# A first stage reordered: half loads, one bank per set, and folds moved between two engines

## The chip, the cores and the metric

The kernel runs on one core of a Trainium2 chip. The metric is the device time of one execution in microseconds (us); lower is better. A core has five engines that work through queues of their own and wait for each other by semaphores: TensorE (PE in the profile, with its weight loads as PEld), VectorE (DVE), ScalarE (ACT), GpSimd (POOL) and SyncE (SP, which here only issues DMAs). ACT and POOL issue some DMAs too. A time "at 14.00" is counted from the start of the profiled span.

## The reference

The kernel computes a Fourier mixing layer and then a gated feed-forward layer. The input `x` is 8 batches of 3008 rows of 256 numbers, in float32:

```python
X = np.fft.fft(x, axis=1)            # over 3008 rows
X = np.fft.fft(X, axis=2)            # over 256 columns
x2 = X.real.reshape(24064, 256)
g = x2 @ w_gate                      # 256 -> 1536
out = (g / (1 + exp(-g)) * (x2 @ w_val)) @ w_out   # 1536 -> 256
```

## The kernel before, in words

The real part of the two transforms is a sum of products of cosines and sines. The cosine and sine over the 256 columns are multiplied into the gate and value weights (`Wp` and `Wq`, and `Wm`, a signed copy of `Wq`), so that the transform over rows is all that is left for the data. A row k and its mirror M-k share their products: `P` (even part) and `Q` (odd part) are computed once, and the two rows come out as `P·Wp + Q·Wq` and `P·Wp + Q·Wm`.

The transform over rows is made small by folding. The 3008 rows are split into four residues ("sets", a = 0 to 3); in each, rising rows are added to falling rows (the mirror), then the columns are folded on themselves into even and odd halves (`EOA`, `EOb`, index `eo`). What is left is multiplied on PE with a table of sines and cosines `Tab`, made on the chip from iotas. A batch has a large part A (128 rows per set) and a rest C (60 rows per set, two sets stacked on one tile).

The kernel has two stages.

*The first stage* (code up to `tmp_ctx.close()`, some 20 us) is written out by hand, engine by engine, in program order. It loads batch 0, builds the tables, folds, transforms, and multiplies the first 512 columns of the gate and value weights. Its steps, by the lines that the profile names:

- `x` loads: the four rising sets in one DMA of 1024 KB (L261), four falling sets of 256 KB each, issued in turn by ACT and SP (`fall_a`, L264), the rising rest (`rises_c`, L267, 512 KB), four falling pieces of the rest (`fall_c`, L270), and row 0 through POOL's queue (L404).
- warm-up: 48 matmuls of a zero tile (L306).
- tables: iotas on POOL (L282 to L288), `turns` on POOL (L364), `angles` and `magnitude` on DVE (L368, L372), sines and cosines on ACT (L375, L378), sign copies on ACT (`opposite`, L384; `weigh_ce`, L387). `putA` and `putC` are permutation matrices: an iota and a comparison (L286 and L355 for A, L301 and L406 for C).
- `place` (L438): a float32 matmul with `putA` or `putC` brings the rising rows of one set into the order of the falling ones, in PSUM.
- folds: DVE adds the falling rows to it. `cross` does it for sets 0 and 1 (L447), and `cross_halves` and `half_fold` for sets 2 and 3 and the rest C (L451, L452, L460), `ends` for the one column left over (L455). POOL folds the columns of sets 0 and 1 in `fold_d` (L497), the odd sums for sets 2 and 3 as well, and adds the odd sums up (L570). ACT casts the even ones to bfloat16 (L500).
- transform: `half_folded` (L488) and `folded_c` (L493) on PE into four accumulators `acc[eo][q]`; `row0` (L628) adds the row 0 terms (`heads`, L464 and L465 on POOL) to the two odd accumulators. ACT copies `acc[eo][0]` to SBUF (`even_copy`, L517), and DVE adds and subtracts it from `acc[eo][1]` to give `P` and `Q` (`first_puts`, L646).
- weights: POOL issues the DMAs, which cast to bfloat16 (`load_w`, L394): chunk 0 of gate and value (`W0`), then chunks 1 and 2 into the space of `XA`. PE multiplies chunk 0 with the cosine and sine tables (`first_w`, L505); ACT and DVE copy the result out (L508). The order is gate first, then value.
- `turn_signs` (L345 to L347) and `row_signs` (L357, L358) make small sign columns.

PSUM has eight banks. In the first stage they are taken from the three pools that the second stage uses (`psG` 3, `psV` 3, `psO` 2).

*The second stage* goes over tiles of 512 columns of `P`, `Q` and 12 blocks of the hidden size each. Its order is made before the program runs by a planner: every operation has an engine, a duration, a due time (`SHIFT` and `BIAS` tables) and dependencies, and the planner writes each engine's queue from these. It starts from fixed assumptions on when the first stage's results are there, and knows nothing of the first stage's code. For the first tiles, a block is: PE multiplies `P·Wp` and `Q·Wq` into a gate and a value bank (L1015), ACT applies the gate function (L1050), DVE multiplies (`hp`, L1053); then PE adds `Q·Wm` terms to the same banks for the mirrored rows, and ACT and DVE do the same again (L1071, L1074). Among them stand the products of weight chunks 1 and 2 (L1501, copied out at L1504, L1507, L1510), and POOL makes `Wm` (L512, L1516). The output product is at L1279.

Of the kernel before, what the change touches and what calls it, by code (L numbers as in the profile page):

```python
# [12 lines left out]
F32 = mybir.dt.float32  # L13
I32 = mybir.dt.int32
BF16 = mybir.dt.bfloat16
AF = mybir.ActivationFunctionType
Alu = mybir.AluOpType

@with_exitstack
def kernel(  # L20
# [8 lines left out]
    nc = tc.nc  # L29
    B, M, D = x.shape  # L30
    Dff = moe_w_gate.shape[1]
    P = 128
# [46 lines left out]
    psG = Slots("psG", 3, space=bass.MemoryType.PSUM)  # L79
    psV = Slots("psV", 3, space=bass.MemoryType.PSUM)  # L80
    psO = Slots("psO", 2, space=bass.MemoryType.PSUM)
# [6 lines left out]
    Tab = const.tile([P, 2, 2, 2, NTAB], BF16, name="Tab")  # L88
    halfpi = const.tile([P, 1], F32, name="halfpi")
# [31 lines left out]

    def up_block(b, j, n):
        return rows_at(b, 2 * j - 1, [[2 * D, n], [R * D, 4], [1, 2 * D]])

    def rows_at(b, row, ap):
        return bass.AP(tensor=x.tensor, offset=(b * M + row) * D, ap=ap)
# [118 lines left out]
    Ec0 = tp.tile([P, 2, 2, 1], F32, name="Ec0")  # L245
# [27 lines left out]
    fall_a(3, nc.scalar)  # L273
    fall_a(2, q)
    fall_a(1, nc.scalar)
    fall_a(0, q)
    rises_c(q)
# [8 lines left out]
    nc.gpsimd.iota(putA, pattern=[[-LA, NA], [1, LA]], base=JA - 1, **iota)  # L286
# [6 lines left out]
    for a in range(2):  # L293
        fall_c(1, a, q)
        fall_c(0, a, q)
# [7 lines left out]
    for i in range(4):  # L303
        ps = psO.tile([P, T], F32, name="o")
        for j in range(12):
            nc.tensor.matmul(ps[:, 0:P], sel, sel, start=True, stop=True)  # L306
# [7 lines left out]
    mm_ = col("mm", 4)  # L314
# [28 lines left out]
    def turn_signs():  # L343
        n_ = col("n_", 4, I32)
        vts(n_, mm_, scalar1=0.5, scalar2=0.25, op0=Alu.mult, op1=Alu.add)  # L345
        vts(n_, n_, scalar1=1, scalar2=None, op0=Alu.bitwise_and)
        vts(turn_sign, n_, scalar1=-2.0, scalar2=1.0, op0=Alu.mult, op1=Alu.add)  # L347
# [7 lines left out]
    vts(putA, putA, scalar1=pcol, scalar2=None, op0=Alu.is_equal)  # L355
# [6 lines left out]
    def turns(t1, kf, ch):  # L362
        for i in range(2):
            pts(t1[:, i, :], kf, scalar1=mM[:, 2 * ch + i:2 * ch + i + 1], scalar2=1.0, op0=Alu.mult, op1=Alu.mult)  # L364
# [21 lines left out]
    def weigh_ce():  # L386
        nc.scalar.activation(Tab[:, 1, 1, :, 0:NCE], Tab[:, 1, 1, :, 0:NCE], AF.Copy, scale=wC)  # L387

    def load_w(c, only):
        for i, src in ((0, moe_w_gate), (1, moe_w_val)):  # L390
            if i not in only:
                continue
            w_ = src.rearrange("(no p) f -> p no f", p=P)[:, :, c * T:(c + 1) * T]
            nc.gpsimd.dma_start(out=Wraw[i][:, :, (c - 1) * T:c * T] if c else W0[i], in_=w_)  # L394
# [11 lines left out]
    pts(putC, putC, scalar1=pcol, scalar2=1.0, op0=Alu.is_equal, op1=Alu.mult)  # L406
    nc.gpsimd.memset(sel[0:1, :], 1.0)
# [22 lines left out]
    weigh_ce()  # L430
    opposite(0)

    def place(X, put, n, pools):
        pss = []
        for a in range(n):
            pool, nm = pools[a % len(pools)]
            ps = pool.tile([P, 2, D], F32, name=nm)
            nc.tensor.matmul(ps.rearrange("p q d -> p (q d)"), put, X[:, a].rearrange("p q d -> p (q d)"),  # L438
                             start=True, stop=True)
            pss.append(ps)  # L440
        return pss

    def falling(X, pss, a):
        return (X[:, 7 - a] if len(pss) == 4 else X[:, 2 + a])[:, ::-1]

    def cross(to, X, pss, a):
        vtt(to[:, :, 1:D], pss[a][:, :, 1:D], falling(X, pss, a)[:, :, D - 1:0:-1], op=Alu.add)  # L447

    def cross_halves(to, X, pss, a):
        down = falling(X, pss, a)  # L450
        vtt(to, pss[a][:, :, 1:P + 1], down[:, :, D - 1:P - 1:-1], op=Alu.add)  # L451
        vtt(pss[a][:, :, P:D], pss[a][:, :, P:D], down[:, :, P:0:-1], op=Alu.add)  # L452

    def ends(to, X, pss, a):
        vtt(to, pss[a][:, :, 0:1], falling(X, pss, a)[:, :, 0:1], op=Alu.add)  # L455
# [3 lines left out]
    def half_fold(eo, to, low, pss, a):  # L459
        vtt(to, low[:, :, ::-1], pss[a][:, :, P:D], op=SUMS[eo])  # L460

    def heads(ev, od, CE):

        ptt(CE[:, :, 0, 0, -1:], ev, od, op=Alu.add)  # L464
        ptt(CE[:, :, 0, 1, -1:], ev, od, op=Alu.subtract)  # L465
# [3 lines left out]
    def warm(n):  # L469
        ps = psO.tile([P, T], F32, name="o")  # L470
        for i in range(n):
            nc.tensor.matmul(ps[:, 0:P], sel, sel, start=True, stop=True)

    def start_acc(eo):
        for q, (pool, nm) in enumerate(((psV, "v"), (psG, "g"))):
            acc[eo][q] = pool.tile([P, T], F32, name=nm)
# [7 lines left out]
    def half_folded(eo, a0, first):  # L484
        for q in range(2):
# [9 lines left out]
    def fold_d(eo, a0):  # L495
        F = FA[:, a0:a0 + 2]
        ptt(EOA[eo][a0 // 2], F[:, :, :, P:0:-1], F[:, :, :, P:D], op=SUMS[eo])  # L497

    def half_cast(eo, a0):
        nc.scalar.copy(EOb[:, eo, a0:a0 + 2], EOA[eo][a0 // 2])  # L500
# [18 lines left out]

    psG.at = psV.at = 2  # L520
    psA = place(XA, putA, 4, ((psG, "g"), (psV, "v")))
    warm(8)
    for a in range(2):
        cross(FA[:, a], XA, psA, a)
    for a in range(2):
        ends(Eh[:, a], XA, psA, a)
# [9 lines left out]
    for a in range(2, 4):  # L536
        ends(Eh[:, a], XA, psA, a)
    start_acc(0)
    start_acc(1)
    psC = place(XC0, putC, 2, ((psO, "o"),))  # L540
# [3 lines left out]
    half_cast(0, 2)  # L544
    nc.scalar.activation(Z0.rearrange("p q k d -> p (q k d)"), zero.to_broadcast([P, 6 * P]), AF.Copy)
    opposite(1)
# [19 lines left out]
    fold_d(1, 2)  # L566
    hd = tp.tile([P, 2, 2, 1], F32, name="hd")
    ptt(hd, Eh[:, 0:2], Eh[:, 2:4], op=Alu.add)
    heads(hd[:, 0], hd[:, 1], CEa)
    ptt(EOb[:, 1, 0:2], EOA[1][0], EOA[1][1], op=Alu.add)  # L570
    half_folded(0, 0, True)
    half_folded(0, 2, False)
    cross_halves(FC[:, 0], XC0, psC, 0)
    half_fold(0, EB[:, 0, 0], FC[:, 0], psC, 0)
    folded_c(0, 0)
    copies = [first_w(0, k, 1, p_.tile([P, T], F32, name=n_)) for k, (p_, n_) in enumerate(((psG, "g"), (psV, "v")))]
    cross_halves(FC[:, 1], XC0, psC, 1)
    half_fold(0, EB[:, 0, 1], FC[:, 1], psC, 1)
    folded_c(0, 1)
    od0 = even_copy(0)  # L580
    for a in range(2):
        half_fold(1, EB[:, 1, a], FC[:, a], psC, a)
    for a in range(2):
        ends(Ec0[:, a], XC0, psC, a)
    for a in range(2):
        folded_c(1, a, True)
    half_folded(1, 0, False)
    load_w(1, (1,))
    heads(Ec0[:, 0], Ec0[:, 1], CEc)
    load_w(2, (0, 1))  # L590
    for k in range(2):
        pts(BBc[:, :, 1, k, 0:1], Ec0[:, 1 - k], scalar1=(nsgn, sgn)[k], scalar2=1.0, op0=Alu.mult, op1=Alu.mult)
    nc.gpsimd.iota(kfO, pattern=[[4, GH]], base=1, **iota)
# [70 lines left out]
    tmp_ctx.close()  # L664

# [1099 lines left out]
```

## Time and profile before

| what | value |
|---|---|
| time before, median of 3 runs | 597.46 us (597.39 to 598.78) |
| the profiled execution's own time | 597.77 us |
| its span | 596.0 us |
| PE busy in the span | 590.9 us, 99% |
| DVE, ACT, POOL busy | 568.6, 553.6 and 533.5 us |
| granted PE clock over the span | 1.0 |

The page lists busy times, a chain of waits followed back from the last instruction, and groups of instructions by line. A row of the timeline gives the start, the duration, the engine, the line, what is written from what, the tile's shape, how many instructions are merged, and in brackets the idle time before it with what ended that. Durations of neighbouring instructions of one engine overlap by some 0.08 us on DVE and 0.1 us on ACT, so what an instruction costs its engine is the distance to the next start.

### The profile page before, as it was taken

The page shows a single profiled execution, that of the slowest core. Times are in us where ns is not written, and L with a number is a line of the kernel's source. Part 1 is how long each engine was busy: PE and PEld are TensorE (multiplying, and loading weights), DVE is VectorE, ACT ScalarE, POOL GpSimd, SP SyncE. Part 2 cuts the span into 40 slices and gives each one's busy share as a digit, 9 for nine tenths or more (in the row PEclk, how much of TensorE's full clock was granted, in tenths as well). Part 3 has the DMA queues.
Part 4 walks back from the last instruction along what each step waited for, and adds up shares of the span by engine and source line. Part 5 has one row for each costly group of instructions (what it writes and reads, how often), then busy time and mean ns, then how long its engine had stood idle before and what let it go on. Part 6 is the DMA issues. An engine that isn't in the chain of part 4 may idle for free.

```text
span 596.0 us, 12394 instructions
## 1 busy us (share of the span) xinstructions
PE 590.9 (99%) x4014; PEld 390.6 (66%) x4014; DVE 568.6 (95%) x1062; ACT 553.6 (93%) x1071; POOL 533.5 (90%) x491
## 2 busy tenths in 40 slices
PE   9999999999999999999999999999999999999997
PEld 6456676666666666666666666666666666666686
DVE  9989999999999999999999999999999999999993
ACT  8768989999998899899999999999999999999995
POOL 9979999999999999999899998999889868687782
PEclk9999999999999999999999999999999999999999
DMA  9976772756244255285125122054121103202212
GB/s 251 161 222 229 185 235 71 194 165 222 82 149 126 73 139 137 68 273 159 54 82 168 37 64 63 19 152 143 46 63 37 47 19 88 67 28 63 60 54 81
DMA packets 61070, 68.17 MB, mean 114 GB/s; under 512 B 6744, under 2 KB 48668, under 8 KB 61006
## 3 DMA queue, kind: packets, MB, share of 16 engines
q1 hardware_dynamic: 57422, 64.44, 36.1%
q0 software_dynamic: 3216, 2.36, 2.9%
q8 instruction: 31, 0.51, 0.4%
q10 hardware_dynamic: 368, 0.59, 0.3%
q14 instruction: 33, 0.27, 0.2%
HBM read 40.21 MB, written 35.43 MB: 127 GB/s over the span
## 4 chain that ended last, share of the span: by engine, by line
PE 96%; DVE 0%; ACT 0%; issue 0%
PE o L1279 41%; PE g L1015 27%; PE v L1015 21%; PE g L1453 2%; PE o L1453 2%; PE v L1279 1%; PE o L1501 1%; PE g L622 0%; PE o L622 0%; PE g L1279 0%; PE o L1582 0%; PE g L1650 0%; DVE Wp L508 0%; ACT es L1289 0%; DVE Qt L646 0%
## 5 line engine op out<-in xcount | busy, mean ns | idle before, releaser
L1226 POOL TENSOR_TENSOR hm<-sv 128x1024 bf16<-128x1024 f32 (+2 forms) x137 | 254.7, 1862 | 32.3 <-ACT sv L1202 12.9
L1218 DVE SCALAR_TENSOR_TENSOR sv<-es,v 128x512 f32<-128x512 f32 (+2 forms) x262 | 174.0, 670 | 5.9 <-PE v L1015 4.3
L1279 PE MATMUL o<-Wo,hm 128*128 128x256 bf16 (+1 forms) x1128 | 163.7, 273 | 0.0
L1279 PE MATMUL o<-Wo,hp 128*128 128x256 bf16 (+1 forms) x1104 | 161.1, 272 | 0.0
L1229 DVE TENSOR_TENSOR hp<-sp,v 128x512 bf16<-128x512 f32 (+2 forms) x228 | 151.6, 671 | 1.9 <-PE v L1015 1.1
L1279 PEld LDWEIGHTS <-hm 128*128 128x128 bf16 (+2 forms) x1140 | 111.9, 98 | 58.0 <-issue 0.6
L1279 PEld LDWEIGHTS <-hp 128*128 128x128 bf16 (+2 forms) x1140 | 111.8, 98 | 55.3 <-issue 0.3
L1202 ACT ACTIVATE sv<-g 128x512 f32<-128x512 f32 (+2 forms) x181 | 119.0, 675 | 3.6 <-PE g L1015 3.1
L1127 ACT ACTIVATE sp<-g 128x512 f32<-128x512 f32 (+2 forms) x181 | 112.1, 621 | 5.9 <-PE g L1015 4.0
L1015 PE MATMUL g<-Pt,Wp 128*128 128x512 bf16 (+2 forms) x288 | 107.5, 374 | 0.0
L1015 PE MATMUL v<-Pt,Wp 128*128 128x512 bf16 (+2 forms) x288 | 106.2, 375 | 0.2 <-DVE Wp L508 0.2
L1015 PE MATMUL g<-Qt,Wq 128*128 128x512 bf16 (+2 forms) x288 | 105.4, 375 | 0.1
L1088 ACT ACTIVATE v<-bc,w 128x512 f32<-128x512 bf16 (+2 forms) x139 | 100.3, 726 | 1.9 <-DVE sv L1218 1.0
L1152 DVE SCALAR_TENSOR_TENSOR es<-bc,w,v 128x512 f32<-128x512 bf16 (+2 forms) x135 | 97.9, 732 | 2.1
L1150 ACT ACTIVATE es<-v 128x512 f32<-128x512 f32 (+2 forms) x139 | 86.0, 621 | 3.2 <-PE v L1015 1.6
L1015 PEld LDWEIGHTS <-Wp 128*128 128x128 bf16 x576 | 56.3, 98 | 26.0 <-DVE Wp L508 1.0
L1015 PE MATMUL g<-Qt,Wm 128*128 128x512 bf16 (+2 forms) x195 | 73.1, 376 | 0.0
L1131 DVE SCALAR_TENSOR_TENSOR sg<-bc,w,g 128x512 f32<-128x512 bf16 (+2 forms) x93 | 67.3, 724 | 1.6 <-PE g L1015 1.4
L1235 POOL TENSOR_TENSOR hp<-sp,pp 128x512 bf16<-128x512 f32 (+1 forms) x46 | 57.2, 1245 | 8.0 <-ACT pp L1232 7.8
L1202 ACT ACTIVATE sv<-sg 128x512 f32<-128x512 f32 (+2 forms) x93 | 63.6, 695 | 0.5 <-DVE sg L1195 0.5
L1195 DVE SCALAR_TENSOR_TENSOR sg<-sg,g 128x512 f32<-128x512 f32 (+2 forms) x93 | 61.6, 663 | 0.2
L1015 PEld LDWEIGHTS <-Wq 128*128 128x128 bf16 x437 | 42.7, 98 | 27.5 <-issue 0.4
(218 smaller groups left out, 788.7 us busy)
## 6 DMA issues: line engine op xcount, KB each, us to landing
out_dram<-ev SPq DMA_DIRECT2D x96, 128.0 KB
XA<-in_x_dram SPq DMA_DIRECT2D x30, 256.0 KB
tA<-in_x_dram SPq DMA_DIRECT2D x28, 256.0 KB
XA<-tA SPq DMA_DIRECT2D x14, 512.0 KB
XC<-in_x_dram SPq DMA_DIRECT2D x28, 120.0 KB
tC<-in_x_dram SPq DMA_DIRECT2D x28, 120.0 KB
XC<-tC SPq DMA_DIRECT2D x6, 480.0 KB
bc<-br SPq DMA_DIRECT2D x19, 128.0 KB
```

Source lines behind the costliest of these rows:

```text
L1015: nc.tensor.matmul(ps[:, :n], Wt[:, gv, fs], src[:, :n], start=start, stop=stop, skip_group_check=True)
L1088: nc.scalar.activation(T_[kv][:, :w], bc[t][:, :w], AF.Copy, scale=w0[:, 1, f:f + 1])
L1127: nc.scalar.activation(sp_to()[:, :w], T_[kg][:, :w], AF.Silu)
L1131: nc.vector.scalar_tensor_tensor(T_[keg][:, :w], bc[t][:, :w], w0[:, 0, f:f + 1], T_[kg][:, :w], op0=Alu.mult, op1=Alu.add)
L1150: nc.scalar.activation(T_[kes][:, :w], T_[kv][:, :w], AF.Copy, scale=2.0 if on_pool(u) > 1 else 1.0)
L1152: nc.vector.scalar_tensor_tensor(T_[kes][:, :w], bc[t][:, :w], w0[:, 1, f:f + 1], T_[kv][:, :w], op0=Alu.mult, op1=Alu.add)
L1195: nc.vector.scalar_tensor_tensor(T_[kgm][:, :w], T_[keg][:, :w], 2.0, T_[kg][:, :w], op0=Alu.mult, op1=Alu.subtract)
L1202: nc.scalar.activation(sv()[:, f % 2, w - 1::-1, 1], T_[kgm if by_dve else kg][:, :w], AF.Silu)
L1218: nc.vector.scalar_tensor_tensor(sv()[:, f % 2, w - 1::-1, 0], T_[kes][:, :w], 2.0, T_[kv][:, :w], op0=Alu.mult, op1=Alu.subtract)
L1226: nc.gpsimd.tensor_tensor(hts_(t)[1][:, f - 1:f + 1, :w], sv()[:, :, :w, 1], sv()[:, :, :w, 0], op=Alu.mult)
L1229: nc.vector.tensor_tensor(hts_(t)[0][:, f, :wp], T_[ksp][:, :wp], T_[kv][:, :wp], op=Alu.mult)
L1279: nc.tensor.matmul(st["ps"][:n, j, :], hts[t][minus][:, f, c:c + n], Wo[:, f, :], start=(f == 0), stop=(f == nF - 1))
```

## The change

Everything changed is in the first stage; in the second, each engine's instructions stand in the same order as before, behind a first stage that ends with some small POOL operations moved to its end.

- The rising rows of batch 0 are loaded in two halves of 512 KB (`rises_a`). ACT issues falling sets 3 and 2; SP issues set 1, then the rising rest, then set 0. Row 0 goes through SP's queue between two pieces of the rest, no longer through POOL's.
- The warm-up is 33 matmuls; 5 more stand behind each pair of placements.
- Each set has a PSUM bank of its own: placements of A in banks 4, 5, 0, 1, of C in 6, 7; accumulators in 2, 3 (even) and 6, 7 (odd); the four products of weight chunk 0 in 0, 1, 4, 5. The pools of the second stage are opened behind the first.
- `putA`: its iota goes behind the first `turns` on POOL, and its comparison from DVE to POOL.
- `opposite(0)` stands ahead of `weigh_ce` on ACT, and `opposite(1)` ahead of the clearing of `Z0`.
- `fold_d(0, 0)` stands ahead of the load of the gate weights, chunk 0; the loads of chunks 1 and 2 follow the last `fold_d` without other POOL work between.
- The sum of the odd folds (L570), `hd` and `heads` go from POOL to DVE, behind the folds of C.
- The odd accumulators are finished one after the other, each with its `row0`, and `even_copy(1)` is issued after the first.
- For the value weights, ACT copies `Wp` and DVE `Wq` (before, DVE `Wp` and ACT `Wq`). `first_puts(1)` for tile 0 is issued between the two.
- `turn_signs`, `row_signs`, two small products of `Ec0`, an iota and the setting of `sel` go to the end of the stage.

```diff
-    q.dma_start(out=XA3[:, 0:4, :], in_=up_block(0, 1, P))
+    def rises_a(a):
+        q.dma_start(out=XA3[:, a:a + 2, :], in_=rows_at(0, R * a + 1, [[2 * D, P], [R * D, 2], [1, 2 * D]]))
...
+    rises_a(0)
     nc.scalar.activation(w0[:, 0, 0:1], zero, AF.Silu)
     fall_a(3, nc.scalar)
-    fall_a(2, q)
-    fall_a(1, nc.scalar)
+    rises_a(2)
+    fall_a(2, nc.scalar)
+    fall_a(1, q)
+    rises_c(q)
     fall_a(0, q)
-    rises_c(q)
...
-    nc.gpsimd.iota(putA, pattern=[[-LA, NA], [1, LA]], base=JA - 1, **iota)
...
-    for a in range(2):
-        fall_c(1, a, q)
-        fall_c(0, a, q)
+    fall_c(1, 0, q)
+    q.dma_start(out=XC0[NCR:64 + NCR + 1:64, 2:4, 0], in_=rows_at(0, 0, [[2 * R * D, 2], [R * D, 2], [1, D]]))
+    fall_c(0, 0, q)
+    for hi in (1, 0):
+        fall_c(hi, 1, q)
...
-    vts(putA, putA, scalar1=pcol, scalar2=None, op0=Alu.is_equal)
...
     turns(ti[0], kf, 0)
+    nc.gpsimd.iota(putA, pattern=[[-LA, NA], [1, LA]], base=JA - 1, **iota)
+    pts(putA, putA, scalar1=pcol, scalar2=1.0, op0=Alu.is_equal, op1=Alu.mult)
     turns(ti[1], kf, 1)
     more_iotas()
-    nc.gpsimd.dma_start(out=XC0[NCR:64 + NCR + 1:64, 2:4, 0],
-                        in_=rows_at(0, 0, [[2 * R * D, 2], [R * D, 2], [1, D]]))
     pts(putC, putC, scalar1=pcol, scalar2=1.0, op0=Alu.is_equal, op1=Alu.mult)
-    nc.gpsimd.memset(sel[0:1, :], 1.0)
...
-    weigh_ce()
     opposite(0)
...
-    psA = place(XA, putA, 4, ((psG, "g"), (psV, "v")))
-    warm(8)
+    for a in range(4):
+        place(bA[a], XA, putA, a)
+        if a % 2:
+            warm(5)
...
-    row_signs()
-    load_w(0, (0,))
-    fold_d(0, 0)
-    load_w(0, (1,))
-    fold_d(1, 0)
-    for a in range(2, 4):
-        cross_halves(FA[:, a, :, 1:P + 1], XA, psA, a)
-    for a in range(2, 4):
-        half_fold(0, EOA[0][1][:, a - 2], FA[:, a, :, 1:P + 1], psA, a)
+    fold_d(0, 0)
+    load_w(0, (0,))
+    fold_d(1, 0)
+    load_w(0, (1,))
+    for a in range(2, 4):
+        cross_halves(FA[:, a, :, 1:P + 1], psA[a], XA[:, 7 - a, ::-1])
+        if a == 2:
+            ends_a(0)
+            ends_a(1)
+        half_fold(0, EOA[0][1][:, a - 2], FA[:, a, :, 1:P + 1], psA[a])
...
+    weigh_ce()
     half_cast(0, 0)
...
-    ptt(hd, Eh[:, 0:2], Eh[:, 2:4], op=Alu.add)
+    vtt(EOb[:, 1, 0:2], EOA[1][0], EOA[1][1], op=Alu.add)
+    vtt(hd, Eh[:, 0:2], Eh[:, 2:4], op=Alu.add)
     heads(hd[:, 0], hd[:, 1], CEa)
-    ptt(EOb[:, 1, 0:2], EOA[1][0], EOA[1][1], op=Alu.add)
+    heads(Ec0[:, 0], Ec0[:, 1], CEc)
...
     first_puts(0, od0, (0, 1))
+    for c in copies:
+        c()
     for i in range(2):
+        half_folded(1, 0, False, (i,))
         row0(0, i, acc[1][i])
+        if i == 0:
+            od1 = even_copy(1)
+    copies = [first_w(1, k, 1 - k, one_bank(4 + k)) for k in range(2)]
     copies[0]()
+    first_puts(1, od1, (0,))
     copies[1]()
-    turn_signs()
-    od1 = even_copy(1)
-    copies += [first_w(1, k, k, psO.tile([P, T], F32, name="o")) for k in range(2)]
-    first_puts(1, od1, (0,))
-    for c in copies[2:4]:
-        c()
     first_puts(1, od1, (1,))
     tmp_ctx.close()
+    first_ctx.close()
+    turn_signs()
+    for k in range(2):
+        pts(BBc[:, :, 1, k, 0:1], Ec0[:, 1 - k], scalar1=(nsgn, sgn)[k], scalar2=1.0, op0=Alu.mult, op1=Alu.mult)
+    nc.gpsimd.iota(kfO, pattern=[[4, GH]], base=1, **iota)
+    nc.gpsimd.memset(sel[0:1, :], 1.0)
+    row_signs()
```

More of the change, by code (lines that the diff above doesn't have):

```diff
@@ L77, in tile, with one_bank @@
             return t
-    psG = Slots("psG", 3, space=bass.MemoryType.PSUM)
-    psV = Slots("psV", 3, space=bass.MemoryType.PSUM)
-    psO = Slots("psO", 2, space=bass.MemoryType.PSUM)
+    first_ctx = ExitStack()
+    banks = [first_ctx.enter_context(tc.tile_pool(name=f"bank{i}", bufs=1, space=bass.MemoryType.PSUM)) for i in range(8)]
+    def one_bank(i):
+        return banks[i].tile([P, T], F32, name=f"b{i}")
+    for i in range(1, 8):
+        one_bank(i)
+    idle = one_bank(0)
     ctx.enter_context(tc.manual_schedule())
@@ L301, in more_iotas, with warm @@
             nc.gpsimd.iota(putC[:, pm - NCR:pm], pattern=[[-2 * LC, NC_], [2, LC]], base=2 * (NCR - LC) + hi, **iota)
[L303 to L306, printed above, removed]
+    def warm(n):
+        for i in range(n):
+            nc.tensor.matmul(idle[:, 0:P], sel, sel, start=True, stop=True)
+    warm(33)
     small = {}
@@ L429 @@
     cosine(1, 0, NCE, ce_angle[1][1])
-    weigh_ce()
     opposite(0)
[L433 to L455, printed above, removed]
+    def place(to, X, put, a):
+        nc.tensor.matmul(to, put, X[:, a].rearrange("p q d -> p (q d)"), start=True, stop=True)
@@ L467, with start_acc, of_sets @@
     acc = [[None, None], [None, None]]
[L469 to L476, printed above, removed]
+    def start_acc(eo, *at):
+        acc[eo] = [one_bank(i) for i in at]
+    def of_sets(bank):
+        return bank.rearrange("p a (q d) -> p a q d", q=2) if len(bank.shape) == 3 else bank.rearrange("p (q d) -> p q d", q=2)
@@ L482, in set_cols, with half_folded @@
         return ps[:, 0:NCE], tab[:, 0:NCE]
-    def half_folded(eo, a0, first):
-        for q in range(2):
+    def half_folded(eo, a0, first, qs=(0, 1)):
+        for q in qs:
             for a in range(a0, a0 + 2):
```

75 lines of the change are left out of this document (42 added, 33 removed).

## The prediction

> **What bounds the kernel now.** I read the page first: busy times, then the chain that ended last.
>
> ```profile
> PE 590.9 (99%) x4014; PEld 390.6 (66%) x4014; DVE 568.6 (95%) x1062; ACT 553.6 (93%) x1071; POOL 533.5 (90%) x491
> ...
> PE 96%; DVE 0%; ACT 0%; issue 0%
> ```
>
> PE is busy for nearly the whole span and makes up the chain. The view by windows says from where on (columns: stretch and length; busy time of PE, PEld, DVE, ACT, POOL with counts; granted PE clock, DMA share, GB/s):
>
> ```profile
> 19.50:24.00 4.50, 4.50 (x22) 2.17 (x23) 4.16 (x11) 3.42 (x7) 4.06 (x8) 1.00 1.03 191
> 24.00:29.50 5.50, 5.50 (x28) 2.54 (x26) 5.50 (x10) 5.05 (x11) 4.75 (x8) 1.00 1.13 161
> 29.50:40.00 10.50, 10.50 (x77) 5.48 (x75) 8.55 (x18) 7.97 (x19) 7.55 (x15) 1.00 0.63 172
> ...
> 19.50:590.00 570.50, 570.49 (x3888) 377.58 (x3889) 550.99 (x992) 537.25 (x1043) 515.37 (x451) 1.00 0.38 111
> ```
>
> From 19.50 to 590 PE is never seen idle, at full clock. The second stage has the same order after the change. So the time can move only by what the first 20 us hand on: the moment when PE gets going, plus any new stall behind it. The second thing to see is DVE: 5.50 busy of 5.50 from 24.00 to 29.50, and only 0.34 idle between 19.50 and 24.00. PE and DVE are both full there, and whoever starts later sets the pace up to 29.5; only from there on has DVE slack (8.55 of 10.50). The chain names what released PE:
>
> ```profile
> 18.67 0.17 DVE Qt L646
> 18.85 0.61 DVE Wp L508
> 19.45 0.05 issue
> 19.50 0.58 PE v L1015 x2
> ...
> 19.71 0.37 PE L1015 MATMUL v<-Qt,Wq 128*128 128x480 bf16 x1
> ```
>
> (The last row is the timeline's, for the second of the two products.) PE waited for DVE to copy the value weights `Wp`, behind `Qt`. That wait is what the change attacks.
>
> **The change, part by part.** *Start of the stage.* The rows:
>
> ```profile
> 1.04 5.30 PE L306 MATMUL o<-sel 128*128 128x128 bf16 x48 [1.04 <-DVE sel L258]
> 6.13 1.36 PE L438 MATMUL g<-XA,putA 128*128 128x512 f32 x2
> ...
> 9.05 1.02 PE L438 MATMUL v<-XA,putA 128*128 128x512 f32 x2
> ...
> 3.50 0.61 DVE L355 TENSOR_SCALAR putA<-putA,pcol 128x128 f32<-128x128 f32 x1
> ...
> 7.35 0.56 DVE L372 TENSOR_SCALAR ra<-rr 128x754 int32<-128x754 int32 x1
> 7.84 0.68 DVE L447 TENSOR_TENSOR FA<-g,XA 128x510 f32<-128x510 f32 x1
> ...
> 6.45 0.84 POOL L406 TENSOR_SCALAR putC<-putC,pcol 128x128 f32<-128x128 f32 x1
> ...
> 2.13 2.86 POOL L364 TENSOR_SCALAR t<-kf,mM 128x377 int32<-128x377 f32 x4
> ```
>
> The warm-up shrinks from 48 to 33 at 0.11, so it ends near 4.6. `putA`: the first half of `turns` is 1.43 on POOL and now starts near 1.9; with an iota of some 0.4 and a comparison as long as that of `putC` (0.84) it is ready at 4.2 to 4.5. The load of 512 KB in place of 1024 KB lands early enough (estimate 4.65: the whole was there by 6.1, and the queue moved 0.39 MB/us):
>
> ```profile
> q1 hardware_dynamic: 190, 0.39, 99.8%
> ...
> q1 hardware_dynamic: 150, 0.25, 98.5%
> q0 software_dynamic: 24, 0.01, 9.3%
> q0 software_dynamic: 169, 0.17, 103.4%
> ```
>
> (DMA by queue, with packets, MB, and share of 16 engines: the first row is the microsecond 3 to 4, the next two 10 to 11, the last 11 to 12.) A placement is two instructions; the four run from 6.13 to 10.07, some 0.86 apart at full clock. [...] On DVE the comparison of 0.53 (0.61 less the overlap) is gone, so `ra` ends and `cross` starts at 7.4, before 7.84: 0.44 gained. Should the comparison take 1.2 on POOL, 0.2 of the total goes back. From there DVE is behind PE and the loads: `cross_halves` of set 3 needs the last falling set, which lands near 10.1 since no byte was saved (98.5% full between 10 and 11), and the folds of C start at 11.5 against 11.71. Row 0, 4 KB, moves to SP between two pieces of C; the POOL issue it leaves is some 0.8 of POOL time. If it lands at 12.5 or the last falling set at 11, I lose 0.9 to 1.0.
>
> *The middle.*
>
> ```profile
> 11.71 0.41 DVE L451 TENSOR_TENSOR FC<-o,XC 128x256 f32<-128x256 f32 x1
> 14.88 0.22 DVE L455 TENSOR_TENSOR Ec<-o,XC 128x2 f32<-128x2 f32 x2
> 15.73 1.20 DVE L646 TENSOR_TENSOR Pt<-g,od 128x188 bf16<-128x188 f32 x5 [0.64 <-ACT od L517]
> 16.92 0.47 DVE L345 TENSOR_SCALAR n__445<-mm 128x4 int32<-128x4 f32 x1
> 17.41 0.17 DVE L346 TENSOR_SCALAR n__445<-n__445 128x4 int32<-128x4 int32 x1
> 17.62 0.55 DVE L347 TENSOR_SCALAR turn_sign<-n__445 128x4 f32<-128x4 int32 x1
> 18.07 0.77 DVE L646 TENSOR_TENSOR Qt<-g,od 128x188 bf16<-128x188 f32 x3
> 18.77 0.68 DVE L508 CAST Wp<-o 128x512 bf16<-128x512 f32 x1
> 19.37 0.49 DVE L646 TENSOR_TENSOR Qt<-g,od 128x84 bf16<-128x84 f32 x2
> ...
> 14.42 1.26 POOL L570 TENSOR_TENSOR EOb<-Fc 128x512 bf16<-128x512 f32 x1
> ```
>
> DVE is through with C at 14.9 (14.88 + 0.22, less the 0.2 above). New on DVE: the odd sum, costed like a `cross` of the same width, 0.60 (0.68 less overlap; the 1.26 of POOL is the far end and would cost 0.6 more on DVE), and five small operations (`hd` and four of `heads`) at 0.11, together 0.46. That makes 15.95 for `Pt`, 0.2 later than before: the wait of 0.64 for ACT pays for most of it. `Pt` takes 1.20, to 17.15. Here `turn_signs` (16.92 to 18.07, 1.15) no longer stands, so `Qt` starts at 17.15 in place of 18.07, 0.9 earlier. `od1` is there by 16.9, as the odd accumulators are finished one by one.
>
> *The weights.* The gate weights' load:
>
> ```profile
> 8.32 0.82 POOL L394 DMA_DIRECT2D W<-in_moe_w_gate_dram  x1
> 9.21 1.08 POOL L497 TENSOR_TENSOR Af<-FA 128x512 f32<-128x512 f32 x1
> ...
> 14.00 0.59 PE L505 MATMUL g<-W,CD 128*128 128x512 bf16 x2
> ```
>
> Its issue moves behind the 1.08 of `fold_d(0, 0)`, to 9.7 or later. Before, it was issued at 8.32 and its queue moved almost nothing until the `x` loads were through at 11; the 0.25 MB then take some 1.5, landing at 13.0 (4.7 behind the issue). Two ends: what counts is the end of the `x` loads, and it lands at 13.0 again; or what counts is 4.7 from the issue, 14.4. I take 13.7, as the queue rows speak for the first and the later issue for some of the second; needed is 13.7, since PE reaches `first_w` a little earlier. The later chunks are issued 1.6 to 1.9 earlier (POOL has the odd sum, `heads`, `row_signs` and one issue less in front), and nothing waited for them. Of the value weights, ACT now copies `Wp`, ending near 18.1, and DVE, through with 0.77 of `Qt` by 17.9, copies `Wq` when PE's product is there, from 17.97 to 18.6. So PE's value products come 1.0 earlier: 18.7 for the second.
>
> *What is next.* DVE, behind `Wq`, does the last of `Qt` (0.49) and then `turn_signs`, which it has not got rid of: 18.57 + 0.47 = 19.04, + 1.15 = 20.19.
>
> ```profile
> 20.17 1.40 DVE L1053 TENSOR_TENSOR hp<-sg,v 128x480 bf16<-128x480 f32 x2 [0.25 <-ACT sg L1050]
> ...
> 25.52 0.94 DVE L372 TENSOR_SCALAR SDf<-XA 128x376 int32<-128x376 int32 x1
> 26.95 0.34 DVE L372 TENSOR_SCALAR SDf<-XA 128x376 int32<-128x376 int32 x1
> ```
>
> The first `hp` starts at 20.19 against 20.17. From here the same DVE work follows without a break up to 29.5. PE may be 1.0 ahead, but its banks come free when DVE has read them, so it waits. What is left is the idle time within the first two `hp`: they take 1.40 where two of them back to back take about 1.20 (0.64 each, 0.08 overlap). That 0.2 was a wait for PE's values through ACT, and it goes. So 20.19 + 1.12 against 20.17 + 1.32: 0.18, say 0.2 gained in total.
>
> `turn_signs` decides this. Three operations on four columns take 0.47, 0.17 and 0.55; 0.17 may be all that they need. With 0.3 to 0.4 for the three, the total gain is 0.9. I take 1.15, because POOL is busy in the new place too (it multiplies `Wm`), and the same operation L372 takes 0.94 or 0.34 at different times in the rows above. [...]
>
> *Moved at no cost.* `opposite(1)` ahead of the clearing of `Z0` on ACT delays SP's clearing of C and the batch 1 loads by some 0.5. Their reader waits on POOL:
>
> ```profile
> POOL SDf L181 <- DVE hp L1053: 2.0, 1, 2.0
> ```
>
> POOL idles 2.0 there for DVE, so 0.5 is covered; with that cover gone it costs 0.5 on POOL, which has 2.95 idle between 29.5 and 40. The two products, the iota, `sel` and `row_signs` run on POOL at the end of the stage, 1.2 in all, ahead of the `Wm` multiplications; these are wanted for the mirrored rows from about 22 on, and POOL has 0.44 idle until 24 besides the time gained in front. The per-set banks free nothing that the chain waited for.
>
> **Sum.** Earlier start of PE 1.0, given back on DVE 0.8: -0.2. The profiled execution took 597.77, 0.31 more than the median 597.46; its durations carry over to the median as they are. 597.46 - 0.2 = 597.3.
>
> **The rivals.** (B) *The gate weights come late.* At 4.7 from the issue they land at 14.4, 0.7 behind their need, and PE, the copies and DVE move by that: -0.2 + 0.75 = +0.55, or +0.85 if the issue slips to 10. For it: the 4.7. Against: the empty queue until 11. 598.0 to 598.3.
>
> [...]
>
> (D) *`turn_signs` is short in its new place*: -0.9, 596.5. For it: 0.17 for L346. Against: 1.15 as measured, and POOL busy.
>
> (E) *Second-stage order in time shifts*: the earlier chunk loads collide with the batch 1 loads (DMA share over 1.0 already from 19.5 to 29.5), or the `x` halves land 1.0 late (+0.9), and more than 1.8 is lost; gains as large need PE to start earlier than the 1.0, and I see no idle time of PE for it.
>
> (F) *The change doesn't do what it says.* PE is released no earlier, as `Wq` waits for PE's product: 0 to +0.3, within the forecast's own range.
>
> **Numbers.** The forecast with F has 0.50, own range 596.9 to 597.8; B 0.15, C 0.12, D 0.15, E 0.08. From 597.46, 0.3% or 1.8 us is about what a measurement of this kernel can tell from no change. A, B, D and F lie within it, and most of C (the rise at 10.1 is +1.4). Beyond it slower: 0.06 of E and 0.03 of C, where both slip; faster: 0.02 of E and 0.01 of D, with all of the start kept and DMAs calmer. The range runs from D's low end, 596.1 (PE's 1.0 and DVE's idle 0.34 ahead of 24.00 both kept), to just above C, 599.1; what lies outside is E and the tails.
>
> **What would show it.** In the profile after: `Qt` near 17.1 and the first value product on `Qt` near 18.7 (right), or still near 19.7 (F); first `hp` near 20.2, DVE full from there to 29.5, with new PE idle time between 19 and 29 of some 0.8 in all that DVE ends. `turn_signs` at 0.4 in all says D. PE's first gate product after 14.2, ended by the weights' DMA, says B. [...] The odd sum over 0.7 on DVE, or `putA` over 1.0 on POOL, puts each its excess on top. The forecast is wrong if PE is idle by more than 1 us after 30, or if DVE has idle time between 21 and 29.

## The result, and the profile after

The changed kernel takes 599.0 us, median of 20 runs (598.35 to 599.84); the kernel before, beside it, 597.62 (597.38 to 598.78). The ratio is 1.002, with a 95% interval of 1.0013 to 1.0027: slower by 1.4 us, where 0.2 us faster was forecast. (The ratios in this document are not the quotients of the two medians given with them.) Measured again, beside its variants, it was 598.46 against 597.63 (1.0012, 1.0003 to 1.002), so slower by 0.8. The profiled execution of the changed kernel took 598.48 in a span of 596.7; it is the third quickest of the 20, and 11 of them took 598.99 or more.

From the page of the changed kernel, busy times and chain:

```profile
PE 590.6 (99%) x4001; PEld 389.0 (65%) x4001; DVE 569.3 (95%) x1067; ACT 554.2 (93%) x1071; POOL 532.2 (89%) x485
...
PE 95%; DVE 2%; POOL 1%; DMA 1%; issue 1%; ACT 0%; POOLq 0%; DVEq 0%; ACTq 0%
```

PE is still busy for 99%, but the chain now has 5% that is not PE: a DMA and POOL (the gate weights and a table, in the first stage), issue time, and DVE. The windows of the changed kernel, with the columns as before:

```profile
16.00:19.50 3.50, 3.50 (x23) 1.58 (x21) 2.60 (x12) 2.20 (x5) 2.86 (x9) 1.00 1.13 171
19.50:24.00 4.50, 4.50 (x22) 1.97 (x21) 4.43 (x14) 3.39 (x7) 3.92 (x7) 1.00 1.05 202
24.00:29.50 5.50, 5.50 (x27) 2.53 (x26) 5.50 (x12) 5.13 (x11) 4.61 (x8) 1.00 1.18 163
```

PE is dense from 16 on (3.50 of 3.50, where before it was busy for 3.13), and the wait for `Wp` is gone. In its place PE's weight loads wait 0.4 for DVE's copy of `Wq`; for `Wp` they waited 1.0 in the first profile of before, and 0.5 in another (`b0_third` below). And what PE does there is late work of the first stage. Timeline rows of the changed kernel (PE, then DVE, then POOL), and how long the two loads of `W` took from issue to landing:

```profile
14.47 0.59 PE L502 MATMUL b<-W,CD 128*128 128x512 bf16 x2 [0.39 <-DMA W<-in_moe_w_gate_dram]
...
17.98 0.60 PE L502 MATMUL b<-W,CD 128*128 128x512 bf16 x2
...
19.80 0.38 PE L1028 MATMUL v<-Qt,Wq 128*128 128x480 bf16 x1
...
16.20 1.20 DVE L647 TENSOR_TENSOR Pt<-b,od 128x188 bf16<-128x188 f32 x5
...
18.16 0.79 DVE L647 TENSOR_TENSOR Qt<-b,od 128x188 bf16<-128x188 f32 x3 [0.69 <-PE b L629]
...
20.14 0.42 DVE L356 TENSOR_SCALAR turn_sign<-mEc 128x4 int32<-128x4 f32 x1
...
21.26 1.21 DVE L1066 TENSOR_TENSOR hp<-sg,v 128x480 bf16<-128x480 f32 x2
...
22.99 1.38 DVE L378 SCALAR_TENSOR_TENSOR XA<-EOf,mM,XA 128x188 f32<-128x188 f32 x4
...
3.63 1.11 POOL L413 TENSOR_SCALAR putA<-putA,pcol 128x128 f32<-128x128 f32 x1
...
10.04 0.97 POOL L404 DMA_DIRECT2D W<-in_moe_w_gate_dram  x1
...
12.08 0.75 POOL L404 DMA_DIRECT2D W<-in_moe_w_val_dram  x1
...
DMA to landing us min/median/max: 4.4/5.0/5.7
```

PE waits 0.39 for the gate weights; the odd products and row 0 stand behind that in PE's queue; DVE waits 0.69 for row 0 ahead of `Qt`, which starts at 18.16 and not at 17.15. The value product on `Qt` is at 19.80, where 18.7 was forecast and 19.71 stood before.

How far one kernel is behind another is read by taking the same matmul in each. Two such matmuls (a `g<-Pt,Wp` near 43 us, a `v<-Qt,Wm` near 570 us) of the changed kernel, then of the first profile of before, then of another profile of before (`b0_third` below, 597.20 us):

```profile
43.57 0.38 PE L1028 MATMUL g<-Pt,Wp 128*128 128x512 bf16 x1
...
570.92 0.30 PE L1028 MATMUL v<-Qt,Wm 128*128 128x328 bf16 x1
```

```profile
43.40 0.38 PE L1015 MATMUL g<-Pt,Wp 128*128 128x512 bf16 x1
...
570.11 0.30 PE L1015 MATMUL v<-Qt,Wm 128*128 128x328 bf16 x1
```

```profile
42.91 0.38 PE L1015 MATMUL g<-Pt,Wp 128*128 128x512 bf16 x1
...
569.56 0.30 PE L1015 MATMUL v<-Qt,Wm 128*128 128x328 bf16 x1
```

Against the first profile of before, the changed kernel is 0.17 behind at 43 us and 0.81 at 570: more than half of what this pair of profiles shows is lost in the second stage, whose order was not changed. And the profile that the prediction was worked out from was itself not the quickest: another execution of the same kernel is 0.49 ahead of it at 43 us. Against that one the first stage loses 0.66 and the second 0.70; 1.36 in all, where the two executions differ by 1.28 (598.48 and 597.20).

### The profile page after: what moved, and what is told of

Read it like the earlier page. It is cut to its first block, busy times and chain, and to the rows that moved or that the text cites. A ratio compares the mean times of both kernels' runs of the same rounds, so it can differ in the third digit from the quotient of the medians.

```text
span 596.7 us, 12370 instructions
## 1 busy us (share of the span) xinstructions
PE 590.6 (99%) x4001; PEld 389.0 (65%) x4001; DVE 569.3 (95%) x1067; ACT 554.2 (93%) x1071; POOL 532.2 (89%) x485
## 4 chain that ended last, share of the span: by engine, by line
PE 95%; DVE 2%; POOL 1%; DMA 1%; issue 1%; ACT 0%; POOLq 0%; DVEq 0%; ACTq 0%
PE o L1292 40%; PE g L1028 27%; PE v L1028 21%; PE g L1466 2%; PE o L1466 2%; DMA W<-in_moe_w_gate_dram 1%; DVE sv L1231 1%; PE v L1292 1%; DVE hp L1242 1%; PE o L1514 1%; POOL t L374 0%; PE g L623 0%; PE o L623 0%; PE b L502 0%; PE g L1292 0%
```

## The experiments

In what follows "lag" is the distance of the same matmul to the first profile of before.

**Undoing two parts.** The first theory puts the loss into the first stage (late gate weights, `turn_signs` ahead of the first `hp`); the second says that the first stage hands on little and the rest comes and goes in the second. `a0_again` is the changed kernel itself.

> The changed kernel unaltered, beside its variants on one chip. First theory (the loss is made in the first 21 us: gate weights late at PE by 0.4, turn_signs of 1.1 between the last Qt and the first hp): first hp near 21.3 against 20.17, the total 1.0 to 1.4 over before, and later in the span no PE wait that before does not have. Second theory (the first stage hands on only 0.2, as the profile at 45 us shows, and the rest are waits of the second stage that come and go): PE's lag behind before at 45 us is 0.1 to 0.4 again, and jumps of 0.2 to 0.3 stand at other places than 174 and 507 us.

`x1_signs`:

```diff
     first_puts(0, od0, (0, 1))
+    turn_signs()
...
-    turn_signs()
```

> turn_signs goes back to its place behind the Pt operations, where the changed kernel's DVE waits 0.69 us for PE. First theory: 0.7 of its 1.1 us falls into that wait, first hp near 20.55, the total 0.5 to 0.8 us below a0_again. Second theory: no more than 0.2 us below it. Rival that turn_signs is hidden anyway by slack in DVE behind 21 us: no difference.

`x2_gate`:

```diff
-    fold_d(0, 0)
     load_w(0, (0,))
+    fold_d(0, 0)
```

> The load of the gate weights goes back ahead of fold_d(0, 0) on POOL, so it is issued near 8.9 us in place of 10.04. First theory: lands 0.4 to 1.1 us earlier, PE's first gate product near 14.08 in place of 14.47, row0 and Qt 0.4 us earlier, the total 0.3 to 0.7 us below a0_again. Second theory: within 0.2 us of a0_again. If the landing is set by the end of the x loads, the product stays at 14.4.

`x3_both` has both edits.

> Both edits. First theory: first hp near 20.1, the total 1.0 to 1.4 us below a0_again, so at or below before. Second theory: at most 0.3 us below a0_again, still about 1 us over before.

| kernel | median us (before beside it: 597.63) | first `hp` at | lag at 25 us | at 160 | at 180 | at 580 |
|---|---|---|---|---|---|---|
| a0_again | 598.46 | 21.58 | 0.48 | 0.51 | 0.83 | 1.49 |
| x1_signs | 598.51 | 20.32 | 0.03 | 0.09 | 0.42 | 0.43 |
| x2_gate | 598.19 | 21.01 | -0.09 | -0.03 | 0.29 | 0.32 |
| x3_both | 598.47 | 20.27 | 0.05 | 0.12 | 0.44 | 0.52 |

Both theories missed, though the totals of `x1_signs` and `x3_both` are what the second had. `x3_both` brings the first `hp` back to where it was, 1.3 earlier, and gains nothing in the median; and `x2_gate`, with its first `hp` 0.74 later than `x3_both`, is ahead of it at 25 us. So the first `hp` doesn't set the pace. By these four profiles the value product on `Qt` does: it stands at 20.12, 19.73, 19.56 and 19.75 in the four, and the lags at 25 us have the same order. Loading the gate weights earlier is worth 0.3 in the median (598.19 against 598.46; the intervals against before, 1.0 to 1.0017 and 1.0003 to 1.002, overlap). And the jumps, which the second theory had at other places, stay: all four, and the first profile of the changed kernel, make a jump of 0.3 at the same two places, near 172 and near 507 us.

The lags at 580 are of single executions, which took 599.11, 598.06, 597.94 and 598.14, so the first stands above its median and the others below theirs. The one of `a0_again` has a step of 0.64 that no other profile shows. An output copy on ACT waits for the DMA that empties its buffer, and PE waits for ACT:

```profile
258.14 0.58 ACT L1299 COPY ev<-o 128x512 f32<-128x512 f32 x1 [0.55 <-DMA out_dram<-ev]
...
258.78 0.60 PE L1292 MATMUL o<-Wo,hp 128*128 128x256 bf16 x4 [0.42 <-ACT ev L1299]
```

How often the changed kernel has such a step isn't shown.

**The two jumps.** DVE's rows around them, of the changed kernel, with PE's rows that follow:

```profile
171.75 0.44 DVE L1483 TENSOR_TENSOR Pt<-g,od 128x272 bf16<-128x272 f32 x1
172.48 0.69 DVE L1231 SCALAR_TENSOR_TENSOR sv<-es,v 128x512 f32<-128x512 f32 x1 [0.29 <-issue]
...
174.45 0.38 PE L1028 MATMUL g<-Pt,Wp 128*128 128x512 bf16 x1 [0.16 <-DVE Pt L1483]
...
504.38 0.75 DVE L1165 SCALAR_TENSOR_TENSOR es<-bc,w,v 128x512 f32<-128x512 bf16 x1
505.45 0.69 DVE L1231 SCALAR_TENSOR_TENSOR sv<-es,v 128x512 f32<-128x512 f32 x1 [0.32 <-PE v L1028]
```

and of the kernel before at the first place:

```profile
171.52 0.43 DVE L1470 TENSOR_TENSOR Pt<-g,od 128x272 bf16<-128x272 f32 x1
171.89 0.69 DVE L1218 SCALAR_TENSOR_TENSOR sv<-es,v 128x512 f32<-128x512 f32 x1
...
174.29 1.07 DVE L1470 TENSOR_TENSOR Qt<-g,od 128x272 bf16<-128x272 f32 x3 [0.48 <-PE g L1015]
```

At the first place DVE stands still for 0.29 with nothing that the profile shows to wait for ("issue"); at the second the profile names PE. Counted from 0 in DVE's records, semaphore instructions included, the two late operations are numbers 447 and 1215 in each profile of the changed kernel, 768 or 6 times 128 apart, each right behind a semaphore instruction. (In the kernel before, number 447 stands behind a semaphore as well: it is the `Qt` of the last row, ahead of which DVE idles 0.48; in the changed kernel the same `Qt`, at 174.32, follows the operation before it without a gap.) The change adds five instructions to DVE in the first stage (the odd sum, `hd` and four of `heads`, less the comparison of `putA`), so every later one moves up by five numbers. The theory, put together from these two numbers: at each 128th instruction DVE pauses, and it costs something only where the instruction ahead of the point is a wait, behind which DVE has nothing in hand. That the distance is 128 was the author's estimate here, as 768 has other divisors too; the late operations of `y1_after_pad1` below, at numbers 575 and 703, speak for it. What makes DVE pause, and that it pauses at the points where no time is lost, was not shown.

`y1_after_pad1`, the changed kernel (`gap` is a tile that both kernels reserve and don't use; here it gets a name):

```diff
-    tp.tile([P, 48], F32, name="gap")
+    gap = tp.tile([P, 48], F32, name="gap")
...
     copies[0]()
+    nc.vector.memset(gap[:, 0:1], 0.0)
     first_puts(1, od1, (0,))
```

> The changed kernel with one 1-element memset more on DVE, put where DVE waits 0.69 us for PE ahead of the first Qt. Theory P (position: DVE pauses some 0.3 to 0.4 us at every 128th of its instructions, and the change, which has five DVE instructions more in the first stage, moves two of these points, rows 447 and 1215, onto a semaphore wait behind which DVE has no spare time): the points move by one, onto the wait itself, which lies under the operation before it; the jumps of 0.3 at 172 and 505 us go, the total is 0.4 to 0.6 us below a0_again's 598.46, near 597.9. Rival: the jumps come from transfers or PSUM banks of the second stage: they stay, and the total is within 0.2 us of a0_again.

`y2_before_pad5`, the kernel before, with the same name for `gap`:

```diff
...
+    for i in range(5):
+        nc.vector.memset(gap[:, i:i + 1], 0.0)
     first_puts(0, od0, (0, 1))
```

> The kernel before with five 1-element memsets more on DVE, where it waits 0.64 us for ACT ahead of the first Pt; nothing else. Theory P: jumps of 0.3 us at 172 and 505 us, as in the changed kernel, and the total 0.4 to 0.6 us above before, near 598.1. Rival: no jump and within 0.1 us of before.

`y3_heads_pool`, on top of `x2_gate`:

```diff
-        vtt(CE[:, :, 0, 0, -1:], ev, od, op=Alu.add)
-        vtt(CE[:, :, 0, 1, -1:], ev, od, op=Alu.subtract)
+        ptt(CE[:, :, 0, 0, -1:], ev, od, op=Alu.add)
+        ptt(CE[:, :, 0, 1, -1:], ev, od, op=Alu.subtract)
...
-    vtt(hd, Eh[:, 0:2], Eh[:, 2:4], op=Alu.add)
+    ptt(hd, Eh[:, 0:2], Eh[:, 2:4], op=Alu.add)
```

> x2_gate with hd and the four operations of heads back on POOL: DVE then has as many instructions as in the kernel before. Theory P: no jumps at 172 and 505 us, the total 0.5 us or more below x2_gate's 598.19, so 597.3 to 597.7, at the level of before. Rival: within 0.2 us of x2_gate. The five operations take 0.46 us on DVE ahead of Pt; if they set the start of the value products, 0.2 to 0.4 us come on top.

Rows of `y2_before_pad5` at the two places:

```profile
173.95 0.69 DVE L1220 SCALAR_TENSOR_TENSOR sv<-es,v 128x512 f32<-128x512 f32 x1 [0.30 <-issue]
...
175.92 0.38 PE L1017 MATMUL g<-Pt,Wp 128*128 128x512 bf16 x1 [0.17 <-DVE Pt L1472]
...
506.77 0.69 DVE L1220 SCALAR_TENSOR_TENSOR sv<-es,v 128x512 f32<-128x512 f32 x1 [0.32 <-PE v L1017]
```

and of `y1_after_pad1` at the first:

```profile
171.61 0.43 DVE L1484 TENSOR_TENSOR Pt<-g,od 128x272 bf16<-128x272 f32 x1
171.98 0.69 DVE L1232 SCALAR_TENSOR_TENSOR sv<-es,v 128x512 f32<-128x512 f32 x1
```

This settles that the jumps come from the place of the operations in DVE's stream. Five memsets in the kernel before, put where DVE idles, bring both, with the same 0.3 in the same operations, and nothing else of that kernel was touched; one more in the changed kernel takes both away, and so does `y3_heads_pool`. Over all runs here the jumps are in each of the seven profiles with five instructions more, and in none of the eight with another count (seven with the count of before, one with six more).

The totals follow only in part. `y2_before_pad5` is 598.05 against 597.77 (1.0008, 0.9999 to 1.0016), 0.3 where 0.4 to 0.6 was expected, and its interval takes in no change. `y1_after_pad1` stays at 598.56 (1.001, 1.0001 to 1.0018), no better than `a0_again`: in its profile (597.94, below that median) two smaller steps, 0.2 each, stand at 237 and 283 us in place of those taken away. Ahead of them DVE is late again:

```profile
228.68 0.69 DVE L1243 TENSOR_TENSOR hp<-sp,v 128x512 bf16<-128x512 f32 x1 [0.29 <-PE o L1293]
...
281.60 1.29 DVE L1243 TENSOR_TENSOR hp<-sp,v 128x512 bf16<-128x512 f32 x2 [0.16 <-PE o L1293]
```

These are its records 575 and 703, so 447 and once and twice 128, each right behind a semaphore; in the changed kernel the same `hp` operations follow the one before them without a gap. The added memset seems to have moved the pauses onto other operations, and not taken them away; that they make the two steps was not tested by a run of its own. `y3_heads_pool` stays at 598.39 (1.001, 1.0002 to 1.0019). Its edit isn't clean: the operations on POOL also put the loads of the later chunks back (the first from 13.61 in `x2_gate` to 15.89), and PE loses 0.5 between 20 and 25 us. Just behind 60 us its lag is 0.66. What happens there is seen at its largest in the profiled execution of `y2_before_pad5`, which took 599.84, 1.8 above its median:

```profile
41.10 2.36 POOL L181 TENSOR_TENSOR SDf<-XC 128x1020 f32<-128x1020 f32 x1 [4.36 <-DVE hp L1055]
...
61.91 0.38 PE L1017 MATMUL v<-Pt,Wp 128*128 128x512 bf16 x1 [1.91 <-ACT v L1090]
```

The first fold of batch 1 on POOL starts at 41.10; before it was 39.17, behind a wait of 1.95. In the profiles of the changed kernel and of `y3_heads_pool` the row names a DMA as what ended that wait (`XC<-tC`). Counted from PE's own stream (the start less the lag at 43 us), the fold may start at 39.2 to 39.3 (first profile of before, `b1_signs_late`) and nothing follows; at 39.9 (`y3_heads_pool`, `b0_second`) PE loses 0.4 at 60 us, at 41.6 (`y2_before_pad5`) 2.1. So it is in an execution of the kernel before and in variants of both kernels, and in none of the three profiles of the changed kernel itself. It widens the spread; that the change makes it more frequent wasn't shown.

**The kernel before again, and one part alone.** `b1_signs_late`:

```diff
     copies[1]()
-    turn_signs()
...
     first_puts(1, od1, (1,))
+    turn_signs()
```

> The kernel before with one part of the change alone: turn_signs goes behind the last Qt. DVE has the same number of instructions, so no jump at 172 or 505 us by theory P. Theory of the prediction (DVE is full from the first hp to 29.5, what is saved ahead of Qt is given back behind it): Qt 0.8 to 1.15 us earlier, first hp where it was, the total within 0.2 us of before. Rival (PE sets the pace to 29.5 and DVE has spare time that its operations hide by running long beside POOL): the value products come 0.5 to 1.0 us earlier and the total is 0.4 to 0.9 us below before.

Two more profiles of the kernel before and one of the changed:

> The kernel before, a second profile. If turn_signs ahead of Qt takes 0.8 to 1.15 us from execution to execution, the second value product on Qt lies between 19.2 and 19.75 and PE at 45 us up to 0.5 us ahead of the first profile; no jump of 0.3 at 172 or 505.

> The kernel before, a third profile, with the same expectation as for b0_second.

> The changed kernel, a third profile. Jumps at 172 and 505 us for the third time by theory P; the gate product at 14.3 to 14.5; PE at 45 us 0.1 to 0.5 us behind the first profile of before.

The kernel before took 597.88 and 597.20, the changed one 598.53. DVE's and PE's rows of `b0_third`:

```profile
16.76 0.20 DVE L345 TENSOR_SCALAR n__445<-mm 128x4 int32<-128x4 f32 x1
...
17.58 0.79 DVE L646 TENSOR_TENSOR Qt<-g,od 128x188 bf16<-128x188 f32 x3
...
19.23 0.37 PE L1015 MATMUL v<-Qt,Wq 128*128 128x480 bf16 x1
...
24.00:29.50 5.50, 5.50 (x28) 2.54 (x26) 5.09 (x9) 5.06 (x11) 5.16 (x9) 1.00 1.21 172
```

In both new profiles `turn_signs` takes 0.82 and not 1.15 (16.76 to 17.58 here), `Qt` starts at 17.6, and the value product on `Qt` is at 19.23 and 19.25; `y2_before_pad5` and `b1_signs_late` have `Qt` and the product there too (19.24 and 19.26). The execution that the prediction started from was the slower of two kinds. And DVE has idle time between 24 and 29.5 (5.09 of 5.50), with PE just as dense: DVE wasn't the bound.

`b1_signs_late` took 598.27 against 597.64 (1.0006, 0.9997 to 1.0015). Rows of it, for DVE, ACT and PE:

```profile
17.61 0.78 DVE L646 TENSOR_TENSOR Qt<-g,od 128x188 bf16<-128x188 f32 x3 [0.75 <-ACT od L517]
...
20.98 1.03 ACT L1050 ACTIVATE sg<-g 128x480 f32<-128x480 f32 x2 [1.99 <-DVE turn_sign L347]
...
21.60 0.36 PE L1015 MATMUL g<-Qt,Wm 128*128 128x480 bf16 x1 [0.50 <-ACT sg L1050]
```

Both its theories missed. With `turn_signs` away, `Qt` still starts at 17.61: it waits for `od1`, so `turn_signs` lay in a wait and its removal is worth nothing. At its new place it stops ACT for 1.99, since the first `sg` waits for it, and the lag goes from -0.45 to 0.49. So this edit is no clean copy of the change. That wait isn't in the changed kernel, which keeps the intermediate column in `turn_sign` itself; that `sg` lies in space which the column gives free is argued from the code, not shown.

**Two more parts alone, in the kernel before.** `z1_copies`:

```diff
-    copies += [first_w(1, k, k, psO.tile([P, T], F32, name="o")) for k in range(2)]
+    copies += [first_w(1, k, 1 - k, psO.tile([P, T], F32, name="o")) for k in range(2)]
+    copies[2]()
     first_puts(1, od1, (0,))
-    for c in copies[2:4]:
-        c()
+    copies[3]()
```

> The kernel before with one part of the change alone: ACT copies the value weights Wp and DVE Wq, and Qt of tile 0 is half written between them. The number of DVE's instructions is as before, so no jumps. In the usual execution of before (second and third profile) PE waits only 0.2 us for Wp ahead of the first value product, as the Qt operations start with od1 at 17.6 whatever turn_signs takes: the value product on Qt 0.1 to 0.2 us earlier than 19.23, the total 0 to 0.2 us below before. The prediction had 1.0 us for the product.

597.46 against 597.55 (1.0009, 0.9996 to 1.0022; one of its twelve runs took 601.54): no difference. The profiled execution had `Qt` at 18.09, as in the first profile of before, and against that one PE is 0.19 ahead at 25 us: the 0.2 of the expectation.

`z2_gate_late`:

```diff
+    fold_d(0, 0)
     load_w(0, (0,))
-    fold_d(0, 0)
+    fold_d(1, 0)
     load_w(0, (1,))
-    fold_d(1, 0)
```

> The kernel before with one part of the change alone: the gate weights' load behind fold_d(0, 0), the value weights' behind fold_d(1, 0), on POOL. If the loads make the first stage's loss: PE waits 0.3 us or more for the gate weights near 14.3 and up to 0.4 for the value weights near 18, the value product on Qt 0.5 to 1.0 us behind 19.23, the total 0.5 to 1.0 us over before, no jumps at 172 and 505. If the odd folds on DVE and the order of row 0 make it: the total within 0.3 us of before.

599.45 against 597.55 (1.0031, 1.0019 to 1.0043), more than expected. PE's rows:

```profile
14.46 0.38 PE L505 MATMUL g<-W,CD 128*128 128x512 bf16 x1 [0.45 <-DMA W<-in_moe_w_gate_dram]
...
20.04 0.37 PE L1015 MATMUL v<-Qt,Wq 128*128 128x480 bf16 x1
...
26.43 0.39 PE L1501 MATMUL o<-XA,CD 128*128 128x512 bf16 x1 [1.46 <-DMA XA<-in_moe_w_gate_dram]
```

The later loads alone give the gate product of the changed kernel (14.46 and 14.47) and put the value product 0.8 behind 19.23, where the changed kernel has 0.57 to 0.99 (19.80 to 20.22). The 1.46 at 26.43, for a later chunk, is most of this run's loss; the changed kernel issues its later gate chunk at 15.34, where it is 17.48 here, and has no such wait. In `a0_third`, as in `a0_again`, PE waits for the value weights as well:

```profile
14.43 0.59 PE L502 MATMUL b<-W,CD 128*128 128x512 bf16 x2 [0.34 <-DMA W<-in_moe_w_gate_dram]
...
18.41 0.59 PE L502 MATMUL b<-W,CD 128*128 128x512 bf16 x2 [0.40 <-DMA W<-in_moe_w_val_dram]
```

No version came out that beats the kernel before.

## Why the prediction was wrong

Three steps failed. Against the profile that the forecast started from, the first of them makes 0.64; the other two miss by 1.1 and some 0.7 in opposite directions. **One is "The second stage has the same order after the change. So the time can move only by what the first 20 us hand on".** The order is the same, but its place in DVE's stream of instructions is not. The term was taken as 0; the two jumps are 0.3 each. Before has a loss of 0.17 at 183 us that the changed kernel lacks, which fits its late `Qt` at 174.29; with that taken off, and with 0.2 in smaller steps, it is 0.64 between 43 and 570 us.

**"Given back on DVE 0.8" is wrong.** DVE full in the windows was read as DVE setting the pace. In the changed kernel the first `hp` is 1.09 later than in the first profile of before, and PE at 43 us only 0.17: 0.92 was made good on DVE. Rows of the changed kernel and of before for the same operations:

```profile
25.98 0.65 DVE L382 TENSOR_SCALAR SDf<-XA 128x376 int32<-128x376 int32 x1
```

```profile
22.09 1.81 DVE L368 SCALAR_TENSOR_TENSOR XA<-EOf,mM,XA 128x188 f32<-128x188 f32 x4
```

The first two `hp` take 1.21 where they took 1.40, the four of L378 (L368 before) 1.38 for 1.81, `SDf` 0.65 for 0.94: 0.19, 0.43 and 0.29, 0.91 in all. Rows that looked busy held time that DVE did not need; what made them long wasn't shown, nor that a busy POOL does it, which was one of the grounds for `turn_signs` at 1.15. PE's lag at its first value products is still there at 25 and 43 us, to 0.07, in every profile where nothing stops PE in between. The step should have been: PE keeps what it gains, and what it loses.

**"Earlier start of PE 1.0" is wrong by 1.1 against the first profile and by 1.6 against the usual execution.** Its parts:

- *Gate weights at 13.7.* They landed 4.4 behind an issue at 10.04, at 14.4: rival B's end of the bound, but with a wait of 0.3 to 0.4 where B had 0.7, since PE came to them at 14.1 and not at 13.7. The choice between the two ends was wrong: of the two rows, the one for the issue decided.
- *Value weights.* Their issue moved from 10.25 to 12.08, and the sum has no term for it. PE waited 0.4 for them in two of three profiles. The prediction followed up the moved issues of the later chunks, but not this one.
- *`Qt` at 17.15.* It started at 18.16, behind 0.69 of waiting for row 0 on PE, which the late weights had pushed back in part: with the gate weights early (`x2_gate`) it started at 17.92. Even without this, `od1` was there only at 17.7 (ACT's copy runs from 17.24 to 17.72), not by 16.9.
- *The 0.9 from `turn_signs`.* In the usual execution (`b0_second`, `b0_third`, `y2_before_pad5`; the first profile and `z1_copies` have the other kind) `turn_signs` lies in the wait for `od1`; `b1_signs_late` shows that taking it out moves `Qt` by nothing. A gap of one profile was taken for the gap of the kernel.
- *The exchanged copies* are worth 0.2 (`z1_copies`). The wait of 0.4 for `Wq`, where the usual execution has 0.5 for `Wp`, is rival F's mechanism.

**Right were** the start (placements from 4.79, behind a warm-up that was to end near 4.6 and a half load that was to land at 4.65; the first two take 2.46, to 7.25), the odd sum on DVE, 0.60, and `turn_signs` at its new place, 1.12 in all, so that rival D fell. The comparison of `putA` took 1.11 on POOL, near the forecast's far end of 1.2, `cross` started at 7.66 rather than 7.4, and the folds of C start at 11.62 rather than 11.5. No run shows what the chance of C and the upper end of the range rest on, a rise of the clock as late as 10.1, at +1.4: the granted clock is 1.00 from the start in the windows of both kernels, and of the changed kernel's four placements the first two take 2.46, from 4.79, and the last two 1.94, from 7.53 to 9.47.

**The sum with the measured terms**, against the usual execution of before: the first stage 0.66 (0.6 to 1.0 by the value product; by `x2_gate` and `z2_gate_late` the loads are the larger part), the second 0.70, in all 1.36 for the profiled pair. Between the medians it is 1.4 in the first measurement and 0.8 in the second. That 1.36 and 1.4 agree is in part chance, since both profiled executions lie below their kernels' medians. That the time fell within the stated range is chance too: its upper part stood for C and for weights so late that they alone give 598.0 to 598.3, and the jumps were in none of the cases. No run undoes the whole loss. What stays open is what the median execution of the changed kernel has beyond these profiles, and why the medians of `y1_after_pad1` and `y3_heads_pool`, without the two jumps, are no lower.

## What to carry to other kernels

A profile is one execution: before a gap of half a microsecond is made the ground of a forecast, a second profile of the same kernel shows whether the gap is always there. Where an engine that is not the bound looks full, take the same instruction in two profiles and see whether its delay reaches the bound. And a change that adds instructions to one engine's queue moves every later one up by as many numbers: five more on DVE brought 0.29 and 0.32 us here, at its records 447 and 1215, in code that wasn't touched.

## What the hardware showed that wasn't expected

DVE stood still for 0.29 and 0.32 us ahead of records 447 and 1215 of the changed kernel, each right behind a semaphore wait, and for 0.29 and 0.16 ahead of 575 and 703 in `y1_after_pad1`; five memsets of one element brought 0.30 and 0.32 to the same two operations in the kernel before (`y2_before_pad5`). The kernel before has such a record too, its `Qt` at 174.29, ahead of which DVE idles 0.48. The same `turn_signs`, three operations on four columns, took 0.82 or 1.15 in executions of one kernel, and up to 1.35 in `b1_signs_late` (19.39 to 20.74). And the time of a weight load from issue to landing grew from 4.7 and 4.8 (the two loads, before) to 5.7 (first profile) and 6.3 (`a0_third`) for the value weights of the changed kernel, while it was 4.4 in both for the gate weights.
